# The experts' first product by Strassen's seven products for two of three token blocks, the second product one block at a time

## Chip, cores and metric

One core of one Trainium2 chip. The metric is the device time of one execution in microseconds (us), the median over runs.

## What is computed

```python
x = attention(q, k, v, proj)          # hashed buckets, 2 x 8 heads, 768 tokens, head 64 -> x [1536, 512]
a, b = x @ w1, x @ w2                 # [1536, 1024]
x = (a * b @ w3) @ w_out              # [1536, 512]
p = domain_probs / (domain_probs.sum(-1, keepdims=True) + 1e-9)
out = 0
for e in range(4):
    h = np.maximum(x @ moe2_w1[e], 0)         # first product, [1536, 1024]
    out += p[:, e:e + 1] * (h @ moe2_w2[e])   # second product, [1536, 512]
```

All of it is float32. The kernel keeps every operand of a large product as two halves, a rounded `hi` and the rest `lo`, and makes three matmuls (hi·hi, hi·lo, lo·hi) for one tile product.

## The kernel before

The 1536 tokens are three blocks of 512 (`blk` 0 to 2). A model width of 512 is 4 tiles of 128 (`KM`), a hidden width of 1024 is 8 tiles (`KF`, index `ff`); two `ff` tiles share one slot of weights, a pair `fp` 0 to 3. One tile product of 128 x 512 outputs over the width of 512 is 4 x 3 = 12 matmuls, each 128 x 128 by 128 x 512.

The stages follow each other on TensorE (PE): attention (to about 298 us of the span); the products with `w1` and `w2` and the product `w3 @ w_out` = W (to about 449); the "H products", (a*b) @ W, block by block (H0, H1, H2, the loop `for blk in range(NB)` with keys `("H", blk, ff)`); then the experts.

- **H products.** A step `ff` takes one tile of a*b from SBUF, ACT writes its `hi` half and DVE its `lo` half into one of two `hl` buffers, and PE adds 12 matmuls into four PSUM banks. At a block's end ACT and DVE read the four banks and write the two halves of the block's x (`XH`, lines 153 and 156).
- **Experts.** For expert, block and `ff`: `up` (key `("U", e, blk, ff)`) is the first product into one of four `u_ps` banks; ACT writes relu's `hi` (L817) and DVE its `lo` (L819) from PSUM into `hl`; `down` (key `("O", ...)`) is the second product, one step behind, into four `o_ps` banks. After 8 steps DVE multiplies with the probabilities and adds into `xa` (L838, L841).
- **Weights.** The experts' weights come by DMA on SP's queue into two `wraw` buffers; POOL makes `hi` (L159) and `lo` (L162) in halves of 128 x 512 (`conv32`). `release` hands a slot that has been read for the last time to the next piece.

The order on every engine is made when the program is built: `op` notes engine, assumed duration, what it needs and a due time, and `emit_all` takes for the engine that is free first the waiting instruction with the earliest due time. On the chip each engine then runs its instructions strictly in that order.

Of the kernel before, what the change touches and what calls it, by code (L numbers as in the profile page):

```python
# [71 lines left out]
def tile_lsh_attention_moe(ctx, tc, qk, v, projc, w1, w2, w3T, w_out, dp, e1, e2, out):  # L72
# [143 lines left out]

    def conv32(n, dst, half, src):
        r = raws[n % NRAW][:, 0:512]

        def hi_():  # L220
            return slots[dst][:, 0, half * 512:(half + 1) * 512]

        def lo_():
# [513 lines left out]
    eq = []  # L737
    for e in range(NE):
        for fp in range(4):
            eq.append((("U", e, fp), w_ff, e1[e], fp))  # L740
            eq.append((("O", e, fp), w_fm, e2[e], fp))
    nq = [0]

    def release(slot, key):
        if nq[0] < len(eq):
            name, fn, src, fp = eq[nq[0]]
            conv_tile(name, slot, fn, src, fp, [key], clock[0])
            nq[0] += 1
# [150 lines left out]
```

## Time and profile before

| what | us |
|---|---|
| median of 3 runs (lowest, highest) | 1017.66 (1017.48, 1018.55) |
| the profiled execution: its time | 1020.02 |
| its span, first to last instruction | 1018.2 |
| PE busy in the span | 999.7 (98%) |
| DVE, ACT, POOL busy | 510.1, 362.5, 307.8 |

A busy PE is the union of its matmuls; matmuls are pipelined, so the mean length of one in the list of groups (389 ns) is longer than the distance from one to the next. In the rows, L147 is the helper that issues every matmul, L153 and L156 the helpers for `hi` and `lo`; groups are told apart by tile names (out<-in), with the number of a buffer left out.

### The profile page before, as it was taken

Reading aid. Unit: us, or ns where it says so; the run is one execution under the profiler, and the core shown is the slowest. Engines: PE = TensorE matmul, PEld = TensorE weight load, DVE = VectorE, ACT = ScalarE, POOL = GpSimd, SP = SyncE. Lnnn points to the kernel's source line nnn. Section 1 sums busy time; section 2 is a strip of 40 time slices with the busy share of each in tenths; the row PEclk is TensorE's granted clock in tenths of the full one; section 3 lists DMA queues with packets and bytes.
Section 4 is the critical chain, followed back from the end, with each engine's and each line's share of the span. In section 5 each row is a group of like instructions: output and inputs, shape, how many; then the busy total and the mean of one; then the engine's idle time right before and its main releaser. Section 6 shows DMA issues by size and latency. Waiting matters only on the chain.

```text
span 1018.2 us, 13166 instructions
## 1 busy us (share of the span) xinstructions
PE 999.7 (98%) x5035; PEld 844.6 (83%) x5035; DVE 510.1 (50%) x948; ACT 362.5 (36%) x669; POOL 307.8 (30%) x351
## 2 busy tenths in 40 slices
PE   7899999999999999999999999999999999999998
PEld 6888888988788888888888888888888888888886
DVE  6889999998599965954312212121121212212122
ACT  5889999988433322432201101101101101101100
POOL 6777788664000000074300064000650005300000
PEclk9999999999999999999999999999999999999999
DMA  6843544320034321332200032000220002001011
GB/s 162 184 128 77 130 121 112 82 80 21 1 116 127 119 94 49 117 103 63 63 1 1 1 93 73 0 1 1 78 88 1 1 1 73 31 1 42 1 42 42
DMA packets 51135, 64.12 MB, mean 63 GB/s; under 512 B 17688, under 2 KB 34072, under 8 KB 51072
## 3 DMA queue, kind: packets, MB, share of 16 engines
q1 hardware_dynamic: 50928, 63.27, 22.0%
q8 instruction: 40, 0.66, 0.3%
q14 instruction: 23, 0.19, 0.1%
q10 hardware_dynamic: 144, 0.01, 0.0%
HBM read 47.22 MB, written 3.15 MB: 49 GB/s over the span
## 4 chain that ended last, share of the span: by engine, by line
PE 82%; DVE 14%; DMA 1%; ACT 1%; issue 1%; POOL 1%; SPq 0%; DVEq 0%; ACTq 0%; POOLq 0%
PE u_ps L147 43%; PE o_ps L147 30%; DVE et L485 5%; DVE e L443 5%; PE s_ps L147 3%; PE pv_ps L147 2%; PE t_ps L477 2%; PE t_ps L147 2%; DVE xa L504 1%; DVE cbuf L211 1%; DMA wraw<-in_w 1%; ACT e L446 1%; DMA kb<-hh 0%; DVE cbuf L203 0%; DVE cbuf L206 0%
## 5 line engine op out<-in xcount | busy, mean ns | idle before, releaser
L819 DVE SCALAR_TENSOR_TENSOR hl<-u_ps,hl 128x512 fp32r<-128x512 f32 x96 | 66.4, 691 | 420.4 <-ACT hl L817 420.4
L817 ACT ACTIVATE hl<-u_ps 128x512 fp32r<-128x512 f32 x96 | 57.4, 598 | 459.3 <-PE u_ps L147 401.9
L147 PE MATMUL u_ps<-xh,slotl 128*128 128x512 f32 x936 | 220.6, 389 | 0.0
L147 PEld LDWEIGHTS u_ps<-xh,slotl 128*128 128x128 f32 x936 | 175.7, 188 | 36.5
L147 PE MATMUL u_ps<-xh,slot 128*128 128x512 f32 x696 | 165.0, 389 | 1.2 <-DVE xh L156 1.2
L147 PE MATMUL o_ps<-slotl,hl 128*128 128x512 f32 x648 | 154.7, 389 | 0.0
L147 PEld LDWEIGHTS u_ps<-xh,slot 128*128 128x128 f32 x696 | 130.6, 188 | 28.7 <-DVE xh L156 1.6
L147 PEld LDWEIGHTS o_ps<-slotl,hl 128*128 128x128 f32 x648 | 121.6, 188 | 25.2
L147 PE MATMUL o_ps<-slot,hl 128*128 128x512 f32 x504 | 119.9, 389 | 0.0
L147 PEld LDWEIGHTS o_ps<-slot,hl 128*128 128x128 f32 x504 | 94.6, 188 | 19.6
L159 POOL TENSOR_SCALAR slot<-wraw 128x512 fp32r<-128x512 f32 x28 | 17.8, 634 | 286.7 <-PE u_ps L147 269.7
L485 DVE TENSOR_TENSOR et<-t_ps,et 128x512 fp32r<-128x512 f32 x144 | 96.6, 680 | 5.8 <-ACT et L483 5.2
L446 ACT ACTIVATE e<-e,sm 128x768 f32<-128x768 f32 x96 | 89.5, 933 | 12.3 <-DVE e L443 11.0
L147 PE MATMUL pv_ps<-et,vv 128*128 128x256 f32 x576 | 92.8, 297 | 0.8 <-DVE xa L504 0.5
L443 DVE TENSOR_SCALAR_CACHE_REDUCE e<-s_ps 128x768 f32<-128x768 f32 x96 | 90.4, 945 | 4.9 <-PE t_ps L477 3.0
L477 PE MATMUL t_ps<-ident,e 128*128 128x128 f32 x576 | 87.0, 279 | 5.7 <-DVE et L485 4.0
L483 ACT ACTIVATE et<-t_ps 128x512 fp32r<-128x512 f32 x144 | 83.0, 592 | 12.5 <-PE t_ps L477 5.7
L159 POOL TENSOR_SCALAR slotl<-wraw 128x512 fp32r<-128x512 f32 x36 | 22.5, 624 | 208.8 <-PE u_ps L147 172.3
L477 PEld LDWEIGHTS t_ps<-ident,e 128*128 128x128 f32 x576 | 66.3, 142 | 15.9 <-DVE et L485 8.5
L147 PEld LDWEIGHTS pv_ps<-et,vv 128*128 128x128 f32 x576 | 76.0, 192 | 3.0 <-DVE xa L504 2.4
L456 POOL TENSOR_SCALAR e<-e,sm 128x768 f32<-128x768 f32 x72 | 65.5, 916 | 17.4 <-DVE sm L461 15.4
L147 PE MATMUL s_ps<-ka,hh 128*128 128x512 f32 x192 | 53.5, 360 | 3.8 <-issue 2.2
(111 smaller groups left out, 1092.9 us busy)
## 6 DMA issues: line engine op xcount, KB each, us to landing
wraw<-in_e SPq DMA_DIRECT2D x64, 256.0 KB
wraw<-in_w SPq DMA_DIRECT2D x16, 512.0 KB
wraw<-in_w3T SPq DMA_DIRECT2D x16, 512.0 KB
r<-in_qk SPq DMA_DIRECT2D x15, 384.0 KB
wraw<-in_w_out SPq DMA_DIRECT2D x8, 512.0 KB
rv<-in_v SPq DMA_DIRECT2D x16, 192.0 KB
out<-xa SPq DMA_DIRECT2D x12, 256.0 KB
ka<-hh SPq DMA_DIRECT2D x15, 192.0 KB
```

Of the source, the lines that this page charges most:

```text
L147: nc.tensor.matmul(out=o, lhsT=l, rhs=r, start=start, stop=stop)
L159: nc.gpsimd.tensor_scalar(out=o, in0=i, scalar1=1.0, scalar2=1.0, op0=ALU.mult, op1=ALU.mult)
L211: lambda: nc.vector.scalar_tensor_tensor(out=f(t), in0=lw.bitcast(U32), scalar=2.0 ** -52, in1=f(t), op0=ALU.mult, op1=ALU.mult)),
L443: op(("mx", u, t), "DVE", 873, lambda ps=ps, m=m, e=e: nc.vector.tensor_scalar(out=e, in0=ps[:, 0:S], scalar1=THR, scalar2=None, op0=ALU.m ...
L446: op(("ex", u, t), "ACT", 921, lambda e=e, m=m, rs=rs: nc.scalar.activation(out=e, in_=e, func=AF.Exp, scale=-1.0, bias=m, accum_out=rs), ...
L456: return "POOL", 872, lambda: nc.gpsimd.tensor_scalar(out=e, in0=e, scalar1=r[:, t:t + 1], scalar2=1.0, op0=ALU.mult, op1=ALU.mult)
L477: nc.tensor.transpose(out=ps[:, k, t * 128:(t + 1) * 128], in_=e_t[2 * (u % ER) + t][:, kt * 128:(kt + 1) * 128], identity=ident)
L483: op(("hi", n), "ACT", 480, lambda ps=ps, et=et: nc.scalar.activation(out=et[:, 0], in_=ps, func=AF.Copy), [("T", u, j), ("pv", n - NET)], Tj)
L485: op(("lo", n), "DVE", 602, lambda ps=ps, et=et: nc.vector.tensor_tensor(out=et[:, 1], in0=ps, in1=f(et[:, 0]), op=ALU.subtract), [("hi", ...
L504: op(("xa", u), "DVE", 340, lambda: nc.vector.tensor_tensor(out=xt[a, h // 2, t0:t0 + 256], in0=pv_ps[0:D], in1=pvs, op=ALU.add), [("po", ...
L817: op(("gh", n), "ACT", 480, lambda n=n, nu_=nu_: nc.scalar.activation(out=hl_t[n % 2][:, 0], in_=u_ps[nu_ % 4], func=AF.Relu), [ku] + hfre ...
L819: op(("uf", nu_), "DVE", 602, lambda n=n, nu_=nu_: nc.vector.scalar_tensor_tensor(out=hl_t[n % 2][:, 1], in0=u_ps[nu_ % 4], scalar=0.0, in ...
```

## The change

The first product of blocks 0 and 1 is now one 2 x 2 product of halves for each pair `fp`: rows are the two `ff` tiles, the inner index is two halves of the width (2 tiles each), columns are the two blocks. Strassen's scheme takes seven products M1 to M7 of 6 matmuls in place of eight. It needs five sums of x-parts (made once, by POOL from float32 copies of x in `G`, then split by ACT and DVE), five sums of weight parts for each pair (DVE, `zf`, split by ACT and DVE) and eight sums of results (DVE, `m_t`). Block 2 keeps the plain first product. The hidden features of blocks 1 and 2 stay in SBUF (`kept`); within the pairs PE makes block 0's second product, and then those of block 1 and of block 2 follow. The weights come in full pieces of 128 x 1024 (`conv_full`).

```diff
-    def conv32(n, dst, half, src):
...
+    def conv_full(name, dst, fn, src, fp, after, raw, z_after=None):
...
+        op(("dh", name), "POOL", 1170, lambda: pool_hi(slots[dst][:, 0], r), got + after, T)
+        op(("dd", name), "POOL", 2420, lambda: pool_lo(slots[dst][:, 1], r, slots[dst][:, 0]), [("dh", name)], T)
...
+            op(("z", name, m), "DVE", 340, go, got + z_after, T)
...
+            op(("zh", name, i), "ACT", dur, lambda i=i, src=src: hi_of(zz(i)[:, 0], src()),
...
+            op(("zl", name, i), "DVE", dur, lambda i=i, src=src: lo_of(zz(i)[:, 1], src(), zz(i)[:, 0]), [("zh", name, i)], T)
...
+    load_u(0, 0, [("W", KF - 1)], [("H", NB - 1, 5), ("W", KF - 1)])
+    load_o(0, 0, [("W", KF - 1)])
...
+            if blk == NB - 1 and ff in (1, 3, 7):
+                load_o(0, min((ff + 1) // 2, 3), [("H", blk, ff - 1), ("H", blk, ff)])
...
+        for d in range(KM):
+            op(("hl", blk, d), "ACT", 480, lambda blk=blk, d=d, hb=hb: hi_of(G[blk][:, d], hb[d]),
...
+        def split(m, k, src, ready):
+            op(("yh", m, k), "ACT", 520, lambda: hi_of(bx(m)[:, 0, k], src()), ready, TX)
+            op(("xd", m, k), "DVE", 602, lambda: lo_of(bx(m)[:, 1, k], src(), bx(m)[:, 0, k]), [("yh", m, k)], TX)
...
+        for m, a, b, o in ((4, x21, x11, ALU.subtract), (3, x12, x22, ALU.subtract), (1, x11, x22, ALU.add),
+                           (7, x21, x22, ALU.add), (6, x11, x12, ALU.add)):
+            for k in range(2):
+                op(("xs", m, k), "POOL", 1225, lambda m=m, a=a, b=b, o=o, k=k: nc.gpsimd.tensor_tensor(
+                    out=xs(m)[:, k], in0=G[a[0]][:, a[1] + k], in1=G[b[0]][:, b[1] + k], op=o),
+                   [("hl", b_, d) for b_ in range(2) for d in range(KM)] + [("xd", x, k) for x in xdone[-2:-1]], TX)
+                split(m, k, lambda m=m, k=k: xs(m)[:, k], [("xs", m, k), ("W", KF - 1)] + after)
...
+                    for i in range(6):
+                        k, c = divmod(i, 3)
+                        a, b = T3[c]
+                        mm(u_ps[n % 4], lhs()[:, a, k], bx(m)[:, b, k], i == 0, i == 5)
...
+            for m, x, lhs in ((4, 0, lambda w=w: w()[:, :, 1, 1]), (3, 1, lambda w=w: w()[:, :, 0, 0])):
+                n, got = mul(m, lhs, have_u)
+                op(("uf", n), "ACT", 480, lambda n=n, x=x: hi_of(m_t[x], u_ps[n % 4]), got + prev, clock[0])
...
+            n, got = mul(1, lambda: z(0), have_z)
+            mix("a1", lambda: m_t[2], 0, n, ALU.add, got + prev + [key("t4")])
+            mix("b1", lambda: m_t[3], 1, n, ALU.add, got + prev + [key("t3"), key("a1")])
+            n, got = mul(2, lambda: z(1), have_z)
+            mix("C21", lambda: m_t[0], 0, n, ALU.subtract, got + [key("a1")])
+            mix("b2", lambda: m_t[3], 3, n, ALU.add, got + [key("b1"), key("C21")])
...
+            n, got = mul(5, lambda: z(2), have_z)
+            mix("C12", lambda fp=fp: kept(1, 2 * fp), 1, n, ALU.subtract, got + old + [key("b1")])
+            mix("a2", lambda: m_t[2], 2, n, ALU.add, got + [key("a1"), key("C12")])
+            n, got = mul(7, lambda: z(3), have_z)
+            mix("C11", lambda: m_t[2], 2, n, ALU.add, got + [key("a2")])
...
+            n, got = mul(6, lambda: z(4), have_z)
+            mix("C22", lambda fp=fp: kept(1, 2 * fp + 1), 3, n, ALU.add, got + old + [key("b2")])
...
+            for ff, n in ((2 * fp + 1, n2), (2 * fp, n1)):
+                put_down(e, 0, ff, n, [("gl", n)], o_ps, last_o[0])
...
+        for blk in (1, 2):
...
+                if blk == 2 and ff % 2 == 1 and e + 1 < NE:
+                    load_o(e + 1, ff // 2, [("O", e, 2, ff - 1), ("O", e, 2, ff)])
```

Slots of the weights are given out in another order, pads in SBUF are resized and the scratch space of generated DMAs is made smaller; up to the end of the product W every engine's order stays.

**DVE in H2** (`hl0`, `hl1` are the two buffers of a step's operand; `xh_0` x-parts; `xa`, `gl` hold tiles of a*b, and in the changed kernel `gl0` the float32 copy of block 1's x). Before:

```order
L156 TENSOR_TENSOR hl0_3038<-xa_74,hl0_3038 128x512
L156 TENSOR_TENSOR xh_0_3022<-u_ps0_3041,xh_0_3022 128x512
L156 TENSOR_TENSOR xh_0_3022<-u_ps1_3042,xh_0_3022 128x512
L156 TENSOR_TENSOR xh_0_3022<-u_ps2_3043,xh_0_3022 128x512
L156 TENSOR_TENSOR xh_0_3022<-u_ps3_3044,xh_0_3022 128x512
L156 TENSOR_TENSOR hl1_3039<-xa_74,hl1_3039 128x512
L156 TENSOR_TENSOR hl0_3038<-xa_74,hl0_3038 128x512
L156 TENSOR_TENSOR hl1_3039<-xa_74,hl1_3039 128x512
L156 TENSOR_TENSOR hl0_3038<-gl4_3034,hl0_3038 128x512
```

Now, from step 1 on (`slot0` and `slotl4` take the sums for M1 and M7, `cbuf` holds POOL's sums, `zf` the sums of weight parts):

```order
L158 TENSOR_TENSOR hl1_3030<-xa_71,hl1_3030 128x512
L158 TENSOR_TENSOR xh_0_3019<-cbuf_70,xh_0_3019 128x512
L158 TENSOR_TENSOR hl0_3029<-gl1_3028,hl0_3029 128x512
L158 TENSOR_TENSOR slot0_62<-cbuf_70,slot0_62 128x512
L158 TENSOR_TENSOR hl1_3030<-gl1_3028,hl1_3030 128x512
L158 TENSOR_TENSOR slot0_62<-cbuf_70,slot0_62 128x512
L158 TENSOR_TENSOR slotl4_3025<-cbuf_70,slotl4_3025 128x512
L158 TENSOR_TENSOR hl0_3029<-gl1_3028,hl0_3029 128x512
L158 TENSOR_TENSOR slotl4_3025<-cbuf_70,slotl4_3025 128x512
L750 SCALAR_TENSOR_TENSOR zf_3036<-wraw0_68 128x256 x5
L158 TENSOR_TENSOR hl1_3030<-gl1_3028,hl1_3030 128x512
```

These eleven rows run from step 3's `lo` half to step 7's, H2's last; between the `hl` rows DVE now splits sums that POOL has made.

**POOL in H1 and H2.** Before, pieces of the experts' weights, two instructions for each half:

```order
L159 TENSOR_SCALAR slotl1_3025<-wraw0_71 128x512
L162 TENSOR_TENSOR slotl1_3025<-wraw0_71,slotl1_3025 128x512
L159 TENSOR_SCALAR slotl1_3025<-wraw1_72 128x512
L162 TENSOR_TENSOR slotl1_3025<-wraw1_72,slotl1_3025 128x512
L159 TENSOR_SCALAR slotl2_3026<-wraw0_71 128x512
```

Now:

```order
L164 TENSOR_TENSOR slot2_64<-wraw0_68,slot2_64 128x1024
L164 TENSOR_TENSOR slotl5_3026<-wraw1_69,slotl5_3026 128x1024
L859 TENSOR_TENSOR cbuf_70<-g0_67 128x512 x2
L859 TENSOR_TENSOR cbuf_70<-gl0_3027 128x512 x2
L161 TENSOR_SCALAR slotl1_3022<-wraw1_69 128x1024
L859 TENSOR_TENSOR cbuf_70<-g0_67,gl0_3027 128x512
L164 TENSOR_TENSOR slotl1_3022<-wraw1_69,slotl1_3022 128x1024
L859 TENSOR_TENSOR cbuf_70<-g0_67,gl0_3027 128x512 x5
L161 TENSOR_SCALAR slotl2_3023<-wraw1_69 128x1024
L164 TENSOR_TENSOR slotl2_3023<-wraw1_69,slotl2_3023 128x1024
```

The ten sums (L859, for M4, M3, M1, M7, M6, two each) stand among pieces of weights of twice the width.

**PE at the end of H2 and in the first pair of expert 0.** Before, H2's last step (its last two banks), two first products of block 0 and the first second product:

```order
L147 MATMUL o_ps2_3047<-hl1_3039,slotl0_3024 128x512 x3
L147 MATMUL o_ps3_3048<-hl1_3039,slotl0_3024 128x512 x3
L147 MATMUL u_ps1_3042<-xh0_66,slot2_64 128x512 x12
L147 MATMUL u_ps2_3043<-xh0_66,slotl4_3028 128x512 x12
L147 MATMUL o_ps0_3045<-slot3_65,hl0_3038 128x512 x3
L147 MATMUL o_ps1_3046<-slot3_65,hl0_3038 128x512 x3
```

Now, from M4 on (`slot1` takes the sum for M6, `slotl0` and `zs` those of weight parts, `xh_1` is block 2's x):

```order
L149 MATMUL u_ps0_3038<-xh0_66,slot2_64 128x512 x6
L149 MATMUL o_ps0_3042<-hl1_3030,slotl3_3024 128x512 x3
L149 MATMUL o_ps1_3043<-hl1_3030,slotl3_3024 128x512 x3
L149 MATMUL o_ps2_3044<-hl1_3030,slotl3_3024 128x512 x3
L149 MATMUL o_ps3_3045<-hl1_3030,slotl3_3024 128x512 x3
L149 MATMUL u_ps1_3039<-xh_0_3019,slot2_64 128x512 x6
L149 MATMUL u_ps2_3040<-slot0_62,slotl0_3021 128x512 x6
L149 MATMUL u_ps3_3041<-xh0_66,slotl0_3021 128x512 x6
L149 MATMUL u_ps0_3038<-xh_0_3019,slotl0_3021 128x512 x6
L149 MATMUL u_ps1_3039<-slotl4_3025,slotl0_3021 128x512 x6
L149 MATMUL u_ps2_3040<-slot1_63,zs_3031 128x512 x6
L149 MATMUL u_ps3_3041<-xh_1_3020,slot2_64 128x512 x12
```

M4 stands ahead of H2's last step; M3, M1, M2, M5, M7 and M6 follow it, then block 2's plain products of 12. The first product of expert 0 that stood between steps 0 and 1 of H2 is gone.

## Rows read from the trace of the kernel before

**Rows 1.** The page's part 1, busy time of the engines.

```profile
PE 999.7 (98%) x5035; PEld 844.6 (83%) x5035; DVE 510.1 (50%) x948; ACT 362.5 (36%) x669; POOL 307.8 (30%) x351
```

**Rows 2.** Busy time in stretches (H1 and H2; experts), instructions in brackets, clock, DMA.

```profile
core 0: us, PE busy (x) PEld busy (x) DVE busy (x) ACT busy (x) POOL busy (x), PEclk, DMA share, GB/s
449.00:495.00 46.00, 46.00 (x204) 38.11 (x203) 23.54 (x26) 14.40 (x24) 27.86 (x28) 1.00 0.25 79
495.00:1018.00 523.00, 519.49 (x2292) 429.95 (x2290) 98.77 (x145) 57.43 (x96) 85.52 (x90) 1.00 0.09 29
```

**Rows 3.** Timeline of PE, H1 to the experts' start: start, us, operation, count.

```profile
448.55 21.94 PE L147 MATMUL u_ps<-hl,slotl 128*128 128x512 f32 x96
470.33 2.88 PE L147 MATMUL o_ps<-hl,slotl 128*128 128x512 f32 x12
473.05 2.88 PE L147 MATMUL u_ps<-xh,slot 128*128 128x512 f32 x12
475.77 19.20 PE L147 MATMUL o_ps<-hl,slotl 128*128 128x512 f32 x84
494.81 2.88 PE L147 MATMUL u_ps<-xh,slot 128*128 128x512 f32 x12
```

**Rows 4.** Groups of instructions, 495 to 1018 us: count | busy us, mean ns | idle before.

```profile
L819 DVE SCALAR_TENSOR_TENSOR hl<-u_ps,hl 128x512 fp32r<-128x512 f32 x95 | 65.7, 691 | 419.4 <-ACT hl L817 419.4
L817 ACT ACTIVATE hl<-u_ps 128x512 fp32r<-128x512 f32 x95 | 56.8, 598 | 457.3 <-PE u_ps L147 401.9 <-PE o_ps L147 55.4
...
L162 POOL TENSOR_TENSOR slotl<-wraw,slotl 128x512 fp32r<-128x512 f32 x25 | 32.3, 1291 | 2.1
...
L159 POOL TENSOR_SCALAR slotl<-wraw 128x512 fp32r<-128x512 f32 x25 | 15.6, 623 | 192.3 <-PE u_ps L147 172.3 <-PE o_ps L147 16.5 <-DMA wraw<-in_e 3.2
```

**Rows 5.** Timeline of DVE in H0 to H2.

```profile
446.75 1.10 DVE L156 TENSOR_TENSOR hl<-xa,hl 128x512 fp32r<-128x512 f32 x1 [2.12 <-ACT hl L153]
...
450.16 1.09 DVE L156 TENSOR_TENSOR hl<-xa,hl 128x512 fp32r<-128x512 f32 x1
...
457.60 1.11 DVE L156 TENSOR_TENSOR hl<-xa,hl 128x512 fp32r<-128x512 f32 x1 [2.03 <-ACT hl L153]
...
468.47 0.69 DVE L156 TENSOR_TENSOR hl<-xa,hl 128x512 fp32r<-128x512 f32 x1 [2.03 <-ACT hl L153]
...
473.91 1.71 DVE L156 TENSOR_TENSOR hl<-xa,hl 128x512 fp32r<-128x512 f32 x1 [1.46 <-ACT hl L153]
...
492.92 0.69 DVE L819 SCALAR_TENSOR_TENSOR hl<-u_ps,hl 128x512 fp32r<-128x512 f32 x1 [0.97 <-ACT hl L817]
```

**Rows 6.** Timeline of POOL at the same moments.

```profile
443.35 0.62 POOL L159 TENSOR_SCALAR slot<-wraw 128x512 fp32r<-128x512 f32 x1 [0.78 <-PE u_ps L147]
...
457.55 0.62 POOL L159 TENSOR_SCALAR slot<-wraw 128x512 fp32r<-128x512 f32 x1
458.25 1.60 POOL L162 TENSOR_TENSOR slot<-wraw,slot 128x512 fp32r<-128x512 f32 x1
...
473.79 1.29 POOL L162 TENSOR_TENSOR slotl<-wraw,slotl 128x512 fp32r<-128x512 f32 x1
...
492.88 1.30 POOL L162 TENSOR_TENSOR slotl<-wraw,slotl 128x512 fp32r<-128x512 f32 x1
```

**Rows 7.** Timeline of ACT at the end of H1.

```profile
468.49 2.64 ACT L153 ACTIVATE xh<-u_ps 128x512 fp32r<-128x512 f32 x4
471.02 0.62 ACT L153 ACTIVATE hl<-xa 128x512 fp32r<-128x512 f32 x1
```

**Rows 8.** Stretches of the attention with PE idle, and those after them (columns as in Rows 2).

```profile
36.20:38.50 2.30, 0.14 (x2) 0.10 (x1) 1.40 (x4) 1.44 (x4) 2.19 (x2) 1.00 1.12 123
39.70:43.10 3.40, 3.40 (x17) 3.31 (x16) 2.22 (x6) 1.63 (x3) 0.90 (x2) 0.50 1.04 276
...
67.00:69.90 2.90, 0.61 (x5) 0.37 (x5) 0.85 (x2) 2.00 (x4) 2.82 (x4) 1.00 0.24 51
70.50:73.80 3.30, 3.30 (x16) 3.11 (x15) 2.54 (x7) 3.17 (x6) 0.54 (x2) 0.50 0.93 259
```

**Rows 9.** Timeline of the end.

```profile
1008.89 5.60 PE L147 MATMUL o_ps<-slot,hl 128*128 128x512 f32 x24
...
1012.49 2.79 DVE L841 SCALAR_TENSOR_TENSOR xa<-o_ps,prob,xa 128x512 f32<-128x512 f32 x4 [2.08 <-PE o_ps L147]
...
1013.27 2.37 SPq L848 DMA_DIRECT2D out<-xa  x4
```

More of the change, by code (lines that the diff above doesn't have):

```diff
@@ L735, in tile_lsh_attention_moe @@
         free_w = [("B", NB - 1, 5), ka, kb_, ("W", 5)]
[L737 to L748, printed above, removed]
+    SX = [E_[0], E_[1], L_[4]]
+    UB = [E_[2], E_[3]]
+    OB = [L_[5], L_[1], L_[2], L_[3]]
@@ new lines, in tile_lsh_attention_moe, with kept, relu_hi @@
+    x_in = [("xd", m, k) for m in range(1, 8) for k in range(2)]
+    load_u(0, 1, [("W", KF - 1)], [("M", 0, 0, m) for m in (1, 2, 5, 6, 7)])
+    last_o[0] = [("hl", NB - 1, d) for d in range(KM)]
+    def kept(blk, ff):
+        return G[ff // 4][:, ff % 4] if blk == 1 else G[2][:, ff] if ff < 4 else f(cbuf.rearrange(
+            "p a b c -> p (a b) c"))[:, ff - 4]
+    def relu_hi(n, key, after, m):
+        op(key, "ACT", 480, lambda: nc.scalar.activation(out=hl_t[n % 2][:, 0], in_=m_t[m], func=AF.Relu), after, clock[0])
@@ new lines, in relu_lo, with combine, gather, acc @@
+    def relu_lo(n, key, after, src):
+        op(key, "DVE", 602, lambda: nc.vector.scalar_tensor_tensor(
+            out=hl_t[n % 2][:, 1], in0=src(), scalar=0.0,
+            in1=f(hl_t[n % 2][:, 0]), op0=ALU.max, op1=ALU.subtract), after, clock[0])
+    def combine(out, a, b, o):
+        nc.vector.tensor_tensor(out=out, in0=a, in1=b, op=o)
+    def gather(e, blk, ps, ko):
+        last = []
+        for tt in range(4):
+            t = blk * 4 + tt
+            p = prob[:, t, e:e + 1]
+            def acc(t=t, tt=tt, p=p):
+                if e == 0:
+                    nc.vector.tensor_scalar(out=xa[:, t, :], in0=ps()[tt], scalar1=p, scalar2=None, op0=ALU.mult)
+                else:
+                    nc.vector.scalar_tensor_tensor(out=xa[:, t, :], in0=ps()[tt], scalar=p, in1=xa[:, t, :],
+                                                   op0=ALU.mult, op1=ALU.add)
+            op(("ox", e, t), "DVE", 602, acc, [ko, ("gdone", 1 + t // KF, t % KF)], clock[0] + 2 * Q)
+            last.append(("ox", e, t))
+            if e == NE - 1:
+                op(("st", t), "SP", 700, lambda t=t: nc.sync.dma_start(
+                    out=out[t * 128:(t + 1) * 128, :], in_=xa[:, t, :]), [("ox", e, t)], clock[0])
+        return last
@@ L856, in tile_lsh_attention_moe @@
+            got = gather(e, blk, (lambda: u_ps) if blk == 1 else (lambda: o_ps), ("O", e, blk, KF - 1))
+            if blk == 1:
+                for (n, _), k in zip(sorted(bank, key=lambda b: b[0] % 4), got):
+                    keys[("uf", n)] = keys[k]
+            else:
+                last_o[0] = got
     with tc.manual_schedule():
```

216 lines of the change are left out of this document (139 added, 77 removed).

## The prediction

> **What bounds the kernel now.** I read four views in this order: the busy times, the same by stretches, the timeline of PE, and then the timelines of DVE, POOL and ACT where the change puts new work. PE is busy for 98% of the span, DVE for half of it [rows 1]. From 495 us to the end PE works 519.5 of 523 us at full clock, while DVE, ACT and POOL are busy for 99, 57 and 86 [rows 2]: in the experts the number of matmuls is the time, and the others have room. PE's pace there is 12 matmuls in 2.72 us (473.05 to 475.77 [rows 3]), 0.2267 us each. The same pace holds through H1 and H2, where PE has no gap either [rows 2, 3]. But in H2 that is closer than the busy times show: a step needs ACT's `hi` and DVE's `lo` half, and one DVE `lo`, 0.69 us long at 468.47 [rows 5], took 1.71 at 473.91, while POOL split weights from 473.79 to 475.08 [rows 6]. It ended 0.54 after POOL's instruction did. The other way round, DVE's `lo` at 457.60 ended at 458.71, 0.54 after POOL's 457.55 + 0.62, and POOL's next, from 458.25, took 1.60 instead of 1.29 [rows 4 to 6]. So a DVE instruction that reads two SBUF tensors and a POOL instruction do not run together here; the later one waits. A DVE instruction with one input in PSUM is free of it: 0.69 at 492.92 beside POOL's at 492.88 [rows 5, 6].
>
> **The change: what it removes.** For each expert and pair, seven products of 6 matmuls replace four of 12: 42 for 48. Sixteen pairs save 96 matmuls, 96 x 0.2267 = **21.8 us**, all on the path, since PE waits for nobody there.
>
> **What it adds in the steady state, at no cost as long as DVE keeps its price.** One pair is now 42 + 24 (block 2) + 24 (second product of block 0) = 90 matmuls, 20.4 us on PE. DVE gets eight sums of results and two `lo` halves, 10 x 0.69 (nearest row: L819, one PSUM input, 0.691 [rows 4]) = 6.9, and five sums of weight parts at half the width, 5 x 0.35, with their two splits, 1.4 + 0.35: 10.4 us in all. Counted from the start of M4, M1 ends at 4.08 and DVE begins at 4.28 (ACT starts 0.20 after a bank's last matmul: bank 0 of H1's last step is done at 470.33 - 3 x 0.68 = 468.29, ACT begins at 468.49 [rows 3, 7]). After four sums, at 7.0, M2's bank is free, which block 2's first product takes at 9.5; after six sums and a `lo`, at 9.1, M5's is free, needed at 12.2; the `hl` pair is ready by 12.2, needed at 15.0. Sums of weight parts start after M6, at 9.7, and are split by 15; M1 of the next pair wants them at 23.1. ACT's seven writes (0.6 each) and POOL's piece (the halves of 0.62 and 1.29 twice [rows 4], 3.8 us) fall in the second half of the pair. In the second products of blocks 1 and 2 a step needs 0.20 + 0.60 + 0.69 and two handovers, about 1.8 of its 2.72. I cost all this at nothing; the margins are 2.5 us or more in a pair, 0.9 in a step.
>
> **H0 to H1.** POOL now takes expert 0's first two pieces at full width from 443.35 on [rows 6]: two `hi` of 1.25, then a `lo` of 2.58 from about 445.9 to 448.5. DVE's `lo` for H1's first step, issued at 446.75 [rows 5], has to wait for that end: ready at 449.0, with 0.2 to hand over 0.65 after H1's start at 448.55 [rows 3]. The `lo` of the next step meets the second piece in the same way, 0.3 more. **+0.9 us**; 0 if the pieces come later.
>
> **H2 is where the price is.** The sums of x-parts begin when ACT has copied H1's four banks, at 471.1 [rows 7], 0.2 later on POOL. Before H2's last step can start, DVE must by its order have made seven `lo` halves, ten splits of sums and five sums of weight parts; POOL must have made eight sums, and a full piece of the second weights stands among them. Each of these reads two SBUF tensors on DVE or SBUF on POOL, so they share the time: DVE 17 x 0.54 + 5 x 0.3 = 10.7, POOL 8 x 1.29 + 3.8 = 14.1, together 24.8. From 471.3 that is 496.1 (+0.2). PE would start that step, after seven steps and M4, at 470.33 + 7 x 2.72 + 1.36 = 490.7: it comes 5.6 late. If M6's two sums and the next piece (2.6 + 3.8) get in between, 12.0 late. Nearer than either is the walk through the two orders, instruction by instruction: steps 3 and 7 wait longest (2 to 3.6 us each), since they stand behind splits whose sums POOL has yet to make. It gives 8.4 where a second DVE instruction goes through while POOL waits, and 10.8 where POOL always comes between; no row shows two such DVE instructions in a row against a waiting POOL. The step between 0 and 1 that gave H2 slack (a first product at 473.05 [rows 3]) is gone too. I take **+9.5**; bounds 0 (nothing is shared, as with PSUM inputs) and 12.0.
>
> The rows above show who waits, but not who is served first. The Trainium skill, page "SBUF — State Buffer", section "Who interferes with whom", says that the order of issue decides which of the two is blocked, for a whole instruction. Taken at its word, POOL comes between any two DVE instructions: 10.8, and the sum below would be 1009.3; by the other reading 8.4 and 1006.9.
>
> **The clock.** Twice in the attention PE was nearly idle for over 2 us (0.14 busy in 2.30 us; 0.61 in 2.90), and right after it the granted clock was 0.50, which is 1.2 GHz, for about 3.4 us [rows 8]. At half clock PE does half, so one such fall costs up to 1.7. The waits in H2 that I walked are of that length. I take one fall that nothing hides, **+1.7**; bounds 0 and three, 5.1.
>
> **Sum.** -21.8 + 0.9 + 9.5 + 1.7 = -9.7. The end stays as it is: last matmul, four accumulations, stores [rows 9]. The profiled execution (span 1018.2, own time 1020.02) would have a span of 1008.5 and a time of 1010.3. The median of the runs shown is 1017.66, 2.4 below the profiled time; the same 9.7 off it gives **1008.0 us**.
>
> **Rivals.**
> - *The sharing in H2 hardly delays PE* (DVE's queue gets through between the sums): late by at most 4 us, no fall of the clock. Between 1017.66 - 21.8 = 995.9 and about 1001. For it: ACT and POOL have idle time in H2, 14 and 28 of 46 us busy [rows 2]. Against it: every step's `lo` in H2 already took 1.71, with one DVE instruction a step, and now there are three to four.
> - *DVE's sums of results pace the pairs; slower than before.* Place: M5's bank, which block 2's second product of a pair takes 12.24 after M4. With a sum at c us it comes free at 4.28 + 6c + 0.7 and is handed over 0.2 later, so PE waits 6c - 7.06 in each of 16 pairs. From c = 1.28 on the 9.7 us are gone; at 1.4 it is 16 x 1.34 = 21.4, 1029. For it: DVE took 1.1 to 1.7 beside POOL [rows 5]. Against it: these sums have one input in PSUM, and such rows stand at 0.69 [rows 4, 5].
> - *Full-width splits in the second product of block 2 hold DVE's `lo` for relu*: it waits up to 2.58, a step then needs 0.2 + 0.6 + 2.58 + 0.54 + 0.3 = 4.2 of 2.72, 1.5 late. Twelve pieces meet that stage (experts 0 to 2), and with DMA between them only one or two in four fall inside it: 3 to 6 hits, 1012 to 1017. Against it: only a `lo` that arrives just after a split has begun waits so long.
> - *The matmuls that go don't count.* They would not if PE waited elsewhere in the experts; it has no idle stretch there to fill [rows 2], so I leave it at almost nothing.
>
> **How the numbers follow.** Forecast (late in H2 by 5 to 12 us, clock included) 0.67; rival one 0.15; rival two 0.05; rival three 0.10; the rest, the change being worth nothing or a wait that I did not see, 0.03. A measurement of this kernel tells 0.2%, about 2 us, from no change: faster means under 1015.6. Faster: 0.67 + 0.15 + two thirds of rival three = 0.89; slower: 0.05 + 0.01 + a part of three = 0.07; same 0.04. The bounds of the terms give 995.9 to 1017.66 - 21.8 + 0.9 + 12.0 + 5.1 = 1013.9. The range leaves out the lowest third of rival one and the upper half of rival three: 998.0 to 1013.5.
>
> **What would show it right or wrong.** Right: PE's timeline of H1 is about 1 us longer; H2 with M4 takes 8 to 13 us more than 23.1, with PE waiting for DVE's `hl`, above all ahead of steps 3 and 7; POOL's sums and DVE's splits there take 1.6 to 2 us each instead of 1.29 and 0.69; a stretch at half clock in or after H2; then pairs of 20.4 us without a wait. Wrong: H2 without a wait (rival one), DVE's sums over 1.2 us and PE waiting for them in each pair (two), waits of PE in block 2's second products (three).

## Result, and the profile after the change

| | before | after |
|---|---|---|
| median, us (lowest, highest) | 1017.6 (1017.5, 1018.6) | 1003.7 (1002.5, 1005.6) |
| the profiled execution: time, span | 1020.02, 1018.2 | 1005.64, 1003.9 |
| H2's first matmul | 470.3 | 469.7 |
| from there to the end of the last matmul | 544.2 | 530.4 |
| of that, waits of PE: H2, later | 0, 0 | 6.5, 1.2 |

The ratio of the times is 0.986 (95% interval 0.985 to 0.988): 13.9 us faster, where 9.7 were forecast. A wait is here the distance of two matmuls' starts less 0.2267, added up from 0.1 on.

In the rows of the changed kernel L149 issues the matmuls, L155 and L158 write `hi` and `lo`, L161 and L164 are POOL's `hi` and `lo`, L859 the sums of x-parts, L881 the sums of results, and L876 relu's `lo`; where an experiment adds lines these numbers are a few higher.

The page's busy times and the largest new group on DVE, the sums of results (count | busy us, mean ns | idle before), answer to [rows 1, 4]:

```profile
PE 977.6 (97%) x4939; PEld 822.7 (82%) x4939; DVE 662.0 (66%) x1194; ACT 432.4 (43%) x779; POOL 313.4 (31%) x297
...
L881 DVE TENSOR_TENSOR m<-m,u_ps 128x512 f32<-128x512 f32 x96 | 62.9, 683 | 138.4 <-ACT m L155 114.7
```

96 matmuls are gone, and a sum costs 0.683 us, as assumed. The timeline of PE (start, us, operation, count, idle before it and what ended that) answers to [rows 3]:

```profile
447.97 21.92 PE L149 MATMUL u_ps<-hl,slotl 128*128 128x512 f32 x96
469.73 8.55 PE L149 MATMUL o_ps<-hl,slotl 128*128 128x512 f32 x37
479.09 3.03 PE L149 MATMUL o_ps<-hl,slotl 128*128 128x512 f32 x12 [0.81 <-DVE hl L158]
483.58 3.04 PE L149 MATMUL o_ps<-hl,slotl 128*128 128x512 f32 x12 [1.46 <-DVE hl L158]
486.98 3.02 PE L149 MATMUL o_ps<-hl,slotl 128*128 128x512 f32 x12 [0.36 <-DVE hl L158]
490.97 2.79 PE L149 MATMUL o_ps<-hl,slotl 128*128 128x512 f32 x11 [0.98 <-DVE hl L158]
...
496.89 2.79 PE L149 MATMUL o_ps<-hl,slotl 128*128 128x512 f32 x11 [1.55 <-DVE hl L158]
...
518.57 2.88 PE L149 MATMUL u_ps<-xh,slot 128*128 128x512 f32 x12
...
538.97 2.88 PE L149 MATMUL u_ps<-xh,slot 128*128 128x512 f32 x12
```

H1 is whole, five steps of H2 (3 to 7) wait for DVE's `lo`, and the pairs follow each other every 20.40 us without a wait. What DVE and POOL do in the middle of H2 (timelines) answers to [rows 5, 6]. POOL:

```profile
476.75 1.73 POOL L859 TENSOR_TENSOR cbuf<-g,gl 128x512 f32<-128x512 f32 x1
478.44 2.85 POOL L164 TENSOR_TENSOR slotl<-wraw,slotl 128x1024 fp32r<-128x1024 f32 x1
481.25 6.82 POOL L859 TENSOR_TENSOR cbuf<-g,gl 128x512 f32<-128x512 f32 x4
```

DVE at the same time:

```profile
477.26 1.77 DVE L158 TENSOR_TENSOR hl<-xa,hl 128x512 fp32r<-128x512 f32 x1
478.96 2.88 DVE L158 TENSOR_TENSOR xh<-cbuf,xh 128x512 fp32r<-128x512 f32 x1
481.76 1.76 DVE L158 TENSOR_TENSOR hl<-gl,hl 128x512 fp32r<-128x512 f32 x1
483.44 1.78 DVE L158 TENSOR_TENSOR slot<-cbuf,slot 128x512 fp32r<-128x512 f32 x1
485.14 1.77 DVE L158 TENSOR_TENSOR hl<-gl,hl 128x512 fp32r<-128x512 f32 x1
```

POOL's sums take 1.7 us there (6.82 for four; one alone is 1.30), DVE's splits 1.77, and one 2.88 behind a full-width piece of POOL's: each waits for the other in turn.

After H2 one wait is left per expert but the last, in block 2's second product. The first of the three, in DVE's timeline:

```profile
615.76 3.41 DVE L876 SCALAR_TENSOR_TENSOR hl<-cbuf,hl 128x512 fp32r<-128x512 f32 x2 [2.03 <-ACT hl L995]
```

And in POOL's:

```profile
614.41 1.06 POOL L161 TENSOR_SCALAR slotl<-wraw 128x1024 fp32r<-128x1024 f32 x1 [3.35 <-DMA wraw<-in_e]
615.55 2.40 POOL L164 TENSOR_TENSOR slotl<-wraw,slotl 128x1024 fp32r<-128x1024 f32 x1
```

Two `lo` for relu take 3.41 us instead of 1.3, since the first came 0.21 after a full-width split had begun; PE stands 0.37 us.

### The profile page after: what moved, and what is told of

Same layout as the page of the kernel before. It is cut to its first block, busy times and chain, and to the rows that moved or that the text cites. A ratio compares the mean times of both kernels' runs of the same rounds, so it can differ in the third digit from the quotient of the medians.

```text
span 1003.9 us, 13346 instructions
## 1 busy us (share of the span) xinstructions
PE 977.6 (97%) x4939; PEld 822.7 (82%) x4939; DVE 662.0 (66%) x1194; ACT 432.4 (43%) x779; POOL 313.4 (31%) x297
## 4 chain that ended last, share of the span: by engine, by line
PE 73%; DVE 18%; ACT 3%; issue 2%; DMA 2%; POOL 1%; SPq 0%; DVEq 0%; ACTq 0%
PE u_ps L149 50%; PE o_ps L149 19%; DVE et L468 5%; DVE e L426 5%; PE t_ps L149 2%; DMA r<-in_qk 1%; ACT e L429 1%; DVE xa L487 1%; PE pv_ps L149 1%; PE t_ps L460 1%; PE s_ps L149 1%; ACT et L466 1%; DVE hl L158 1%; DVE xh L158 1%; DVE hl L876 1%
## 5 line engine op out<-in xcount | busy, mean ns | idle before, releaser
L149 PE MATMUL u_ps<-xh,slot 128*128 128x512 f32 x768 | 179.9, 389 | 1.2 <-DVE xh L158 1.2
L149 PE MATMUL o_ps<-slotl,hl 128*128 128x512 f32 x768 | 178.2, 390 | 0.4 <-DVE hl L876 0.2
L149 PEld LDWEIGHTS u_ps<-xh,slot 128*128 128x128 f32 x768 | 144.1, 188 | 31.5 <-DVE xh L158 1.6
L149 PEld LDWEIGHTS o_ps<-slotl,hl 128*128 128x128 f32 x768 | 143.9, 188 | 31.5 <-DVE hl L876 1.7
L881 DVE TENSOR_TENSOR m<-m,u_ps 128x512 f32<-128x512 f32 x96 | 62.9, 683 | 138.4 <-ACT m L155 114.7
L161 POOL TENSOR_SCALAR slot<-wraw 128x1024 fp32r<-128x1024 f32 x16 | 17.3, 1080 | 384.6 <-DVE slotl L158 184.1
L149 PE MATMUL u_ps<-xh,slotl 128*128 128x512 f32 x480 | 111.6, 389 | 0.0
L149 PEld LDWEIGHTS u_ps<-xh,slotl 128*128 128x128 f32 x480 | 90.1, 188 | 18.7
L429 ACT ACTIVATE e<-e,sm 128x768 f32<-128x768 f32 x96 | 89.6, 934 | 12.3 <-DVE e L426 10.8
L149 PE MATMUL pv_ps<-et,vv 128*128 128x256 f32 x576 | 91.8, 295 | 0.9 <-DVE xa L487 0.7
L149 PE MATMUL u_ps<-slotl,hl 128*128 128x512 f32 x384 | 87.7, 389 | 0.0
L149 PEld LDWEIGHTS u_ps<-slotl,hl 128*128 128x128 f32 x384 | 72.1, 188 | 15.0
L149 PEld LDWEIGHTS pv_ps<-et,vv 128*128 128x128 f32 x576 | 75.0, 190 | 3.4 <-DVE xa L487 2.8
L155 ACT ACTIVATE m<-u_ps 128x512 f32<-128x512 f32 x32 | 19.1, 598 | 107.0 <-PE u_ps L149 107.0
L873 ACT ACTIVATE hl<-m 128x512 fp32r<-128x512 f32 x32 | 20.3, 633 | 92.3 <-DVE m L881 92.3
L876 DVE SCALAR_TENSOR_TENSOR hl<-gl,hl 128x512 fp32r<-128x512 f32 x32 | 23.8, 742 | 54.3 <-ACT hl L995 46.2
```

The lines of the kernel that those rows point to most:

```text
L149: nc.tensor.matmul(out=o, lhsT=l, rhs=r, start=start, stop=stop)
L155: nc.scalar.activation(out=dst, in_=ps, func=AF.Copy)
L429: op(("ex", u, t), "ACT", 921, lambda e=e, m=m, rs=rs: nc.scalar.activation(out=e, in_=e, func=AF.Exp, scale=-1.0, bias=m, accum_out=rs), ...
L873: op(key, "ACT", 480, lambda: nc.scalar.activation(out=hl_t[n % 2][:, 0], in_=m_t[m], func=AF.Relu), after, clock[0])
L876: op(key, "DVE", 602, lambda: nc.vector.scalar_tensor_tensor(out=hl_t[n % 2][:, 1], in0=src(), scalar=0.0, in1=f(hl_t[n % 2][:, 0]), op0=A ...
L881: nc.vector.tensor_tensor(out=out, in0=a, in1=b, op=o)
```

## Experiments

The times of one kernel's executions spread by 1 to 5 us here, so the waits and the stretch from H2's first matmul to the end of the last are compared beside the medians. In us:

| kernel | median (runs) | stretch | waits in H2 | later waits |
|---|---|---|---|---|
| the change | 1003.7 (4) | 530.4 | 6.5 | 1.2 |
| c0, the change again | 1003.3 (4) | 530.2 | 6.5 | 1.1 |
| e1, sums of x-parts on DVE | 1002.8 (4) | 528.4 | 2.7 | 2.9 |
| e2, fills in their place | 1002.5 (1) | 525.0 | 1.2 | 1.2 |
| e3, pieces after H2 | 1001.8 (4) | 528.1 | 4.3 | 1.2 |
| e4, three sums of results more | 1007.6 (1) | 534.5 | 6.5 | 4.9 |
| e5, six more | 1042.3 (1) | 569.1 | 6.5 | 39.1 |
| e6, plain products | 1024.6 (5) | 546.2 | 0.5 | 1.4 |
| e7, splits in halves | 1001.5 (4) | 529.1 | 6.4 | 0 |
| e8, e1 + e3 + e7 | 995.4 (5) | 523.4 | 0 | 1.0 |

### c0: the change again

No edit.

> The changed kernel once more, unaltered, beside the experiments of the same call. Its median should be within 0.3% of 1003.7 us. Its trace is to show where the runs' spread (1002.45 to 1005.64) lies: if in H2, the waits there (6.5 us in the trace at hand) are by 1 to 2 us another sum; if in the attention, H1 starts elsewhere than at 447.97.

The waits in H2 are the same, step by step; H2 begins 2.5 us earlier, at 467.19. Across the kernels of this table it begins between 466.8 and 472.0, with the same program before the H products. The difference is there in the first 60 us (busy time by stretches, columns as in [rows 2]). The change:

```profile
20.00:60.00 40.00, 35.27 (x254) 31.82 (x255) 32.67 (x70) 32.80 (x66) 32.11 (x38) 1.00 0.65 152
```

Its repeat, c0:

```profile
20.00:60.00 40.00, 37.58 (x266) 33.57 (x267) 35.14 (x72) 34.70 (x69) 32.62 (x39) 1.00 0.70 164
```

PE is busy for 35.3 or 37.6 of these 40 us. So a spread of some 2 us is the attention's, and the stretch behind H2's start repeats to 0.2.

### e1: the sums of x-parts on DVE

```diff
-                op(("xs", m, k), "POOL", 1225, lambda m=m, a=a, b=b, o=o, k=k: nc.gpsimd.tensor_tensor(
+                op(("xs", m, k), "DVE", 620, lambda m=m, a=a, b=b, o=o, k=k: nc.vector.tensor_tensor(
```

> The ten sums of x-parts are made by DVE instead of POOL; nothing else. Theory (the wait in H2 is DVE and POOL excluding each other, 1.74 and 1.77 us an instruction instead of 1.29 and 0.69): one sum then costs DVE about 0.7 us and keeps nobody else waiting; DVE has at most 27 x 0.69 + 5 x 0.35 = 20.4 us of work for H2's 21.8, only the pieces of the second weights still collide: 4 to 6 of the 6.5 us go, 998 to 1000. Rival (the wait is the length of the chain sum, hi, lo, in a fixed order, whoever makes the sum): DVE's queue grows by ten instructions, the steps' lo stand behind more, and the time stays or rises, 1003 to 1007.

H2's waits fall from 6.5 to 2.7, though DVE has nine instructions more there (one of the ten sums runs in H1). That speaks for the sharing, but it does not show it alone: the planner changed PE's order too. In e1, as in e8 to e11, M4 stands behind step 2 of H2 and M3 ahead of step 7, where the change has M4 ahead of step 7 and M3 behind it; e2, e3 and e7 keep the change's order. M4's own wait in H2 is the first row below, and the second is new: the first pair now waits for DVE (waits of PE: us in total, times, longest; the view counts from a matmul's modelled end, so its times are shorter than those of the table):

```profile
PE u_ps L149 <- DVE xh L158: 1.8, 1, 1.8
PE u_ps L149 <- DVE m L881: 1.3, 1, 1.3
PE o_ps L149 <- DVE hl L158: 0.2, 1, 0.2
```

This second wait comes from a row on POOL (timeline) that no theory had:

```profile
481.74 10.60 POOL L161 TENSOR_SCALAR slotl<-wraw 128x1024 fp32r<-128x1024 f32 x1 [4.58 <-PE o_ps L149]
492.43 3.24 POOL L164 TENSOR_TENSOR slotl<-wraw,slotl 128x1024 fp32r<-128x1024 f32 x1
```

A piece that takes 1.05 took 10.60, so POOL's work for the second weights was moved from H2 into the first pair, where it held DVE. In that time DVE ran its two-input instructions one behind the other; its next 0.19 us of rest, at 491.43, let POOL in. Of 3.7 us won 1.6 came back, and the 1002.8 us miss the 998 to 1000 expected.

### e2: fills instead of the sums

```diff
-                op(("xs", m, k), "POOL", 1225, lambda m=m, a=a, b=b, o=o, k=k: nc.gpsimd.tensor_tensor(
-                    out=xs(m)[:, k], in0=G[a[0]][:, a[1] + k], in1=G[b[0]][:, b[1] + k], op=o),
+                op(("xs", m, k), "POOL", 1225, lambda m=m, a=a, b=b, o=o, k=k: [
+                    nc.gpsimd.memset(xs(m)[:, k], 0.0) for _ in range(2)],
```

> Leaves the ten sums of x-parts out: in the place of each, POOL fills the same tile with zeros twice, so the order, the waits and the place of the splits stay as they are. A fill of this size reads nothing; from the trace's fills of 256 columns (0.31 us) two of 512 take about 1.2 us, close to the 1.29 of a sum. Theory one a (POOL excludes DVE only where it reads SBUF): DVE's splits fall to 0.69 to 0.8 us and 4 to 6 of H2's 6.5 us go. Theory one b (any POOL access of SBUF excludes DVE): the fills take 1.5 to 2 us a pair beside DVE's 1.2 to 1.8 and at most 2 us go. Rival (the chain's length in a fixed order): as the chain is as long as before, at least 5 us of waiting stay.

This kernel leaves the sums out and keeps the change's order on PE, DVE and ACT through H2. POOL's timeline:

```profile
482.32 5.33 POOL L860 MEMSET cbuf<- 128x512 f32 x10
```

DVE's at the same moments:

```profile
482.86 0.68 DVE L158 TENSOR_TENSOR hl<-gl,hl 128x512 fp32r<-128x512 f32 x1
483.46 0.68 DVE L158 TENSOR_TENSOR slot<-cbuf,slot 128x512 fp32r<-128x512 f32 x1
484.07 0.68 DVE L158 TENSOR_TENSOR hl<-gl,hl 128x512 fp32r<-128x512 f32 x1
```

Fills of 0.53 us and splits of 0.68 run side by side, neither longer; 5.3 of H2's 6.5 us go. Two fills are 0.2 us shorter than a sum, for eight sums in H2 some 1.7 us at most, too little for that. So it is not the chain's length, and what excludes DVE is POOL's reading. The Trainium skill, page "SBUF — State Buffer", section "Who interferes with whom", says just that: a DVE instruction with two SBUF inputs contends with a GpSimd instruction that reads SBUF, not with one that only writes it. The rows agree.

### e3: the second weights' pieces after H2

```diff
-            if blk == NB - 1 and ff in (1, 3, 7):
-                load_o(0, min((ff + 1) // 2, 3), [("H", blk, ff - 1), ("H", blk, ff)])
...
+    for fp in (1, 2, 3):
+        load_o(0, fp, [("H", NB - 1, KF - 1), ("zl", ("U", 0, 0), 1)])
```

> Pieces two to four of expert 0's second weights are loaded and split after H2 instead of during it; POOL then has only the sums in H2. Theory (shared access): the two DVE instructions that took 2.6 to 2.9 us behind a full-width piece are back at 0.7 to 1.8, POOL's sums follow each other sooner: 2 to 3 of the 6.5 us go, 1001 to 1002; if the late pieces keep the first expert's second product waiting, that is given back where block 0's second product reads them. Rival (the chain of sums alone): under 0.5 us.

2.2 us of the waits go, as expected, and nothing is given back: the pairs of expert 0 run without a wait. The sums alone still alternate with DVE's splits (1.7 and 1.77 us).

### e4, e5: DVE's sums made longer

```diff
+            ex = []
+            for i in range(3):
+                op(key(f"x{i}"), "DVE", 602, lambda n=n: combine(m_t[2], m_t[0], u_ps[n % 4], ALU.add),
+                   got + prev + [key("t4")] + ex, clock[0])
+                ex = [key(f"x{i}")]
-            mix("a1", lambda: m_t[2], 0, n, ALU.add, got + prev + [key("t4")])
+            mix("a1", lambda: m_t[2], 0, n, ALU.add, got + prev + [key("t4")] + ex)
```

In e5 the 3 is a 6.

> In every pair DVE makes the first sum of results three times more (the same result in the same tile), all with one input in PSUM. In a row such sums follow each other every 0.60 us in the trace of the change, so a pair's sums come 1.8 us later. By the banks: M1's must be free for M6, 8.15 us after M4's start, and is free at 5.6 + 1.8 + 0.2; M2's for block 2's first product at 9.5, free at 6.9 + 1.8 + 0.2. Theory (DVE's sums have room): no wait of PE in the pairs, the stretch from H2's end to the end grows by under 1 us. Rival (the sums already pace the pairs): 16 x 1.8 = 29 us more.

> As before with six repeats: a pair's sums come 3.6 us later. M1's bank is then free for M6 at 5.6 + 3.6 + 0.2 = 9.4 instead of 8.15: PE waits about 1.3 us for DVE ahead of M6 in each of 16 pairs, 20 us in all, 1020 to 1026 in total. If the margin is wider than worked out, under 5; if the wait is handed on to later steps of the pair as well, 16 x 1.8 to 16 x 2.7, 30 to 43.

e4: the stretch is 4.2 us longer, 0.24 in each pair, where under 1 us was expected. e5: 38 us more, 16 times 2.0 ahead of M6, where 1.3 was expected, and 0.4 ahead of block 2's first product. The waits of PE in e5:

```profile
PE u_ps L149 <- DVE m L881: 27.0, 16, 1.7
```

One of them in PE's timeline:

```profile
528.80 1.65 PE L149 MATMUL u_ps<-slot,zs 128*128 128x512 f32 x6 [1.69 <-DVE m L881]
```

The repeats write the tile that the one before wrote, and such sums follow each other every 0.72 us, not 0.60; the delay was 2.17 and 4.33, not 1.8 and 3.6. With that, M1's bank is free for M6 at 5.6 + 4.33 + 0.2 = 10.1, 2.0 after 8.15: as measured, so the room there is 8.15 - 5.8 = 2.35 us. By that e4 would not wait; in it and in e5 the planner put one more sum ahead of the one that frees M2's bank, and the small wait is there. So DVE does not set the pairs' time; the theory holds but for the 0.24, and the rival (29 us in e4) falls.

### e6: plain first products, the rest of the change kept

```diff
-            for m, x, lhs in ((4, 0, lambda w=w: w()[:, :, 1, 1]), (3, 1, lambda w=w: w()[:, :, 0, 0])):
...
+            for blk, ff, nn, hf in ((0, 2 * fp + 1, n2, h2free), (0, 2 * fp, n1, h1free), (1, 2 * fp, 0, 0), (1, 2 * fp + 1, 0, 0)):
...
+                        mm(u_ps[n % 4], w()[:, a, kt // 2, ff % 2, kt % 2], XH[blk][:, b, kt], i == 0, i == 3 * KM - 1)
```

> The first product of blocks 0 and 1 again as four products of 12 matmuls a pair, with no sums of x-parts, of weight parts or of results; the order of the blocks, the kept features in SBUF and block 0's and 1's second products stay as in the change. Theory (the gain is the 96 matmuls and H2's waits are the price of the sums): H2 runs without a wait, 6.5 less, and the experts take 21.8 more: 15 us more than the changed kernel, 1018 to 1020, the time of the kernel before. Rival (the other order of blocks and second products gives part of the gain, or the matmuls removed count for less): a time below 1014.

1024.6, 1.0055 of the kernel before (1.0037 to 1.0073): the other order by itself gains nothing. The stretch is 15.8 longer than the change's, where 15.3 were expected, so the matmuls are worth what was counted. The time misses the 1018 to 1020 expected; it is 21.3 above c0's: 15.8 here, 2.9 of waits in H1, and 2.6 that lie ahead of it or in runs without a trace (the profiled one took 1021.2). H1's waits, in PE's timeline:

```profile
448.30 0.50 PE L149 MATMUL u_ps<-hl,slotl 128*128 128x512 f32 x1 [0.56 <-ACT hl L155]
450.54 19.09 PE L149 MATMUL u_ps<-hl,slotl 128*128 128x512 f32 x83 [1.73 <-DVE hl L158]
```

What DVE does there:

```profile
446.20 3.68 DVE L158 TENSOR_TENSOR xh<-g,xh 128x512 fp32r<-128x512 f32 x4 [2.45 <-ACT xh L155]
```

And POOL:

```profile
445.12 2.40 POOL L164 TENSOR_TENSOR slot<-wraw,slot 128x1024 fp32r<-128x1024 f32 x1
```

Here POOL's full-width `lo` does hold DVE at the start of H1, as the prediction had it for the change, and four splits then stand ahead of the step's `lo`.

### e7: POOL's splits in halves

```diff
-        op(("dh", name), "POOL", 1170, lambda: pool_hi(slots[dst][:, 0], r), got + after, T)
-        op(("dd", name), "POOL", 2420, lambda: pool_lo(slots[dst][:, 1], r, slots[dst][:, 0]), [("dh", name)], T)
+        for i, c in enumerate((slice(0, 512), slice(512, 1024))):
+            dep = [("dd1", name)] if i else got + after
+            op(("dh", name, i), "POOL", 550, lambda c=c: pool_hi(slots[dst][:, 0, c], r[:, c]), dep, T)
+            op(("dd" if i else "dd1", name), "POOL", 1225, lambda c=c: pool_lo(
+                slots[dst][:, 1, c], r[:, c], slots[dst][:, 0, c]), [("dh", name, i)], T)
```

> POOL splits each weight piece in halves of 512 columns (hi, lo, hi, lo) instead of at full width; nothing else. Theory: no DVE instruction waits longer than about 1.8 us; the hits of 2.6 to 2.9 in H2 and in block 2's second products go, and with the latter PE's three waits there: 1 to 2 us less from H2's start to the end. Rival (what counts is how much POOL works, not its longest piece): H2 the same within 0.5 us, and the three waits stay or become others.

The three waits in block 2's second products are gone (block 2 of expert 0, one piece of timeline without a wait), so the length of the pieces made them; H2 keeps 6.4 us, so there it is the sum of POOL's work that counts.

```profile
598.58 21.92 PE L149 MATMUL o_ps<-slotl,hl 128*128 128x512 f32 x96
```

### e8: the three edits together

The edits of e1, e3 and e7.

> The three edits that took waits away, together: the sums of x-parts on DVE, pieces two to four of expert 0's second weights after H2, POOL's splits in halves. With no POOL work in H2, DVE has 27 x 0.60 + 5 x 0.34 = 18 us there for PE's 21.8. Theory: all waits of the change's trace go (6.5 us in H2, 1.2 in block 2's second products, worked out as gaps between matmuls): from H2's start to the last matmul 523 instead of 530.3, a median of 996 to 998. Rival (each cure moves the wait into the first pair, as with the sums on DVE alone, where 1.5 us came back there): 525 to 527, 999 to 1001.

995.4 us (994.8 to 998.3), 0.978 of the kernel before (0.975 to 0.980), and below the change; the stretch is the 523 expected. PE has e1's order here, M4 behind step 2, so the gain is that of the three edits with this order. H2 with M4 and M3 now runs through (timeline of PE), and one wait of 0.9 is left in the first pair:

```profile
467.59 8.32 PE L149 MATMUL o_ps<-hl,slotl 128*128 128x512 f32 x36
475.75 1.52 PE L149 MATMUL u_ps<-xh,slot 128*128 128x512 f32 x6
477.11 11.04 PE L149 MATMUL o_ps<-hl,slotl 128*128 128x512 f32 x48
...
508.38 2.56 PE L149 MATMUL o_ps<-slotl,hl 128*128 128x512 f32 x10 [0.74 <-DVE hl L879]
```

Against c0 the waits taken away are 7.6 - 1.0 = 6.6 of the 6.8 us by which the stretch is shorter.

### e9, e10, e11: who is served

e9 has the edits of e1 and e7; e10 is e1 again; e11 is e1 with a fill:

```diff
+        if name == ("O", 0, 2):
+            op(("dh", name), "POOL", 1170, lambda: [nc.gpsimd.memset(f(slots[dst][:, 0, 0:256]), 0.0),
+                                                    pool_hi(slots[dst][:, 0], r)], got + after, T)
```

> Sums of x-parts on DVE and POOL's splits in halves, with the pieces of the second weights still in H2. It asks who is served when POOL waits while DVE has instructions with two SBUF inputs in a row. If such a row keeps POOL out as it did once (10.60 us instead of 1.05 for one POOL instruction, beside 17 DVE instructions in a row), a POOL half of 0.6 or 1.3 us is to be seen with 5 us or more in H2. If that was a matter of one moment, POOL's halves take at most 1.8 and DVE's instructions beside them 1.2 to 1.8.

> The kernel with the sums of x-parts on DVE and nothing else, again. If DVE's row of instructions keeps POOL out by rule, the second piece's hi in H2 takes 8 us or more once more and the first pair again waits 1 to 2 us; if it was chance, it takes 1.05 to 1.6 and H2's waits are others.

> The kernel with the sums of x-parts on DVE, and one fill of 128 x 256 (0.31 us) more on POOL just ahead of the one instruction that DVE's row kept out for 9.6 us in two runs; the fill writes part of the tile that this instruction writes next. There POOL had come 0.04 and 0.08 us before the running DVE instruction let go (0.14 us before its recorded end, by where POOL's waits ended elsewhere); with the fill it comes about 0.3 us later in the row, some 0.3 us before the next one does. Theory (the moment of arrival decides: POOL is served next when it has waited for 0.1 us or more, and is kept out when it comes shorter before): the instruction takes 1.1 to 1.7 us instead of 10.6, and a DVE instruction beside it 1.5 to 1.8. Rival (a row of DVE instructions that has run for seven or more without a pause keeps POOL out whenever it comes): 9 to 10 us once more.

e10 (1004.5 us, stretch 528.4) shows the hold again, 10.64 us, with the same waits. In e11 (1002.1, 528.4) the fill ran 4.4 us ahead and delayed nothing, since the wait that counts stands behind it; POOL came as close to a hand-over as before, and the hold is there a third time (timeline of POOL):

```profile
477.86 0.31 POOL L742 MEMSET slotl<- 128x256 f32 x1
482.56 10.54 POOL L161 TENSOR_SCALAR slotl<-wraw 128x1024 fp32r<-128x1024 f32 x1 [4.39 <-PE o_ps L149]
```

So it is no chance, but the two readings are not told apart: in all three POOL came within 0.08 us of one DVE instruction's end of reading (taken as 0.14 us before its recorded end, see the last section), and DVE had run seven in a row. Where POOL came at least 0.13 us before that end while DVE's next two-input instruction stood ready, some 90 times in the traces of this case, it was served next; but no row had then been longer than five. Some ten times it came 0.05 us or less before it, behind a single DVE instruction, and was served too: the moment without a row does not keep it out. A long row with POOL coming in good time is in no trace.

e9 (1001.0, 528.3) has no such hold, its longest POOL half took 2.14; its POOL pieces came at other moments. It shows something else, the clock (stretches; PEclk is third from the end):

```profile
475.00:480.00 5.00, 2.54 (x8) 1.59 (x7) 5.00 (x6) 2.82 (x5) 2.64 (x3) 0.84 0.37 105
480.00:485.00 5.00, 5.00 (x13) 3.92 (x12) 5.00 (x9) 2.43 (x4) 0.00 (x0) 0.50 0.00 0
```

PE stood for 0.50 us at 475.9 and, after one matmul, for 2.40 at 476.6. From 479.6 on the matmuls follow each other every 0.427 us instead of 0.227, up to 485.18: 13 x 0.2 = 2.6 us more.

## Why the prediction was right, and which terms were not

- **The matmuls, -21.8: right.** The stretch is 13.8 us shorter, that is -21.8 + 6.5 + 1.2 within 0.3; e6 gives them back. Another 0.6 us is the attention's, where two executions differ by more. The other terms below were 5.6 us too high and 1.2 too low, 4.4 in all where 1008.0 to 1003.7 is 4.3; H2's lateness fell where the forecast had it, between 5 and 12.
- **The pairs at no cost: right**, 20.40 us without a wait. The narrowest margin, M1's bank for M6, was left out of the walk; by e5 it is 2.35, where 2.5 or more was said. Rival two's mechanism exists, but its price, a sum of over 1.28 us, does not: 0.683.
- **H0 to H1, +0.9: 0.** The step that failed is the time at which POOL begins. It was taken from the kernel before [rows 6], two `hi` from 443.35 on; in the change the two `lo` run from 441.14 to 445.90 (POOL's timeline), 0.28 before DVE's `lo` at 446.18. e6 shows the mechanism where a piece comes later.

```profile
441.14 2.39 POOL L164 TENSOR_TENSOR slot<-wraw,slot 128x1024 fp32r<-128x1024 f32 x1
443.50 2.40 POOL L164 TENSOR_TENSOR slotl<-wraw,slotl 128x1024 fp32r<-128x1024 f32 x1
448.17 2.99 POOL L859 TENSOR_TENSOR cbuf<-g 128x512 f32<-128x512 f32 x2 [2.27 <-ACT g L155]
...
469.93 2.99 POOL L859 TENSOR_TENSOR cbuf<-gl 128x512 f32<-128x512 f32 x2 [18.77 <-ACT gl L155]
```

- **H2, +9.5: 6.5.** The mechanism is shown by e2, with the order of PE, DVE and ACT unchanged, and by e3; e1 and e8 fit it. The size failed at "the sums of x-parts begin when ACT has copied H1's four banks": M4's two need block 0's copy alone and ran in H1 (third row above), 2 x 1.3 = 2.6 of work that needs no place in H2. And M3's begin 0.2 after H2's start (last row above), not 0.97 as 471.3 after 470.33 is, since the first of them needs no copy of the fourth bank: 0.8 more. 9.5 - 2.6 - 0.8 = 6.1. That these two are the difference is worked out, not tried. Who is served first is not what was off: in H2 POOL waited for one DVE instruction at a time, as the walk that gave 10.8 had it. The places were half right: steps 3 to 7 waited 1.1, 1.7, 0.6, 1.3 and 1.8, where 3 and 7 were to wait longest, 2 to 3.6 each. Rival one, at most 4, needs what e1, e2 and e8 did: POOL's sums not reading there.
- **The clock, +1.7: 0.** The granted clock was 1.00 through H2 (PEclk below is third from the end); the waits were 0.6 to 1.8 us, with a step or more of matmuls between them. That such a fall was to be reckoned with is shown by e9, where it came after waits of 0.50 and 2.40 with one matmul between them; there it cost 2.6, more than the 1.7 read from [rows 8].

```profile
470.00:495.00 25.00, 21.39 (x91) 16.36 (x89) 23.92 (x18) 11.51 (x20) 21.62 (x12) 1.00 0.07 21
```

- **Full-width splits in block 2's second product, at nothing: +1.2.** Rival three's mechanism was there, three hits (e7 takes them away), but a hit cost 0.4 to 0.5 and not 1.5, though DVE's `lo` took 2.05 longer in the first (2.74 instead of 0.69). The chain of "0.2 + 0.6 + 2.58 + 0.54 + 0.3 = 4.2 of 2.72" was too long, and what it may take was set too short: ACT begins at 615.10, when the step before begins on PE, and the second `lo` ends 3.4 later, at 618.50; the first matmul that reads it is the third of its step, due at 618.30.

## To carry to other kernels

A scheme that saves matmuls moves its cost to where its operands are made: count DVE's two-SBUF-input instructions and POOL's reading ones in that stage as one engine, and move the sums to the one that does them faster, even if it is the busier. Where one engine can keep another from a short instruction, cut the long instruction (e7), and move what isn't due yet out of the full stage (e3). Where the order of the engines is planned, an edit to one engine can move the others' instructions (e1): compare the orders before giving the edit the credit. For effects under 2 us compare the same stretch of two traces, not the medians.

## What was not expected of the hardware

- DVE's row of two-input instructions can keep POOL out for as long as the row lasts: 9.6, 9.6 and 9.5 us beyond the 1.05 of the instruction (e1, e10, e11). The Trainium skill, page "SBUF — State Buffer", section "Who interferes with whom", says that the order of issue decides who blocks; here DVE instructions issued after POOL's went ahead of it, so the rule alone does not tell it. When this happens is left open.
- The excluded one gets in about 0.14 us before the recorded end of the other: in those 90 cases POOL's length was its own plus the time up to that point, within 0.02 us.
- Two sums on DVE that write the same tile start 0.72 us apart, two that write different ones 0.60 (e4, e5); why was not tried.
